# A recurrent attention with a squared-ReLU MLP on one core: a new constant set-up, a new order of the planned work, and stores that two queues may issue

## The chip, the cores and the metric

The kernel runs on one core of one Trainium2 chip. The metric is device time in microseconds (us), the median of several executions. The profile used below is of one execution, taken on the same core; its own time and its span stand in the table further down.

## The reference

The first half is a linear recurrence per batch b and head h (4 batches, 8 heads, 768 time steps, 48 channels a head); the second half is an MLP without a bias whose activation is the square of a ReLU.

```
for t in range(S):
    cur = einsum('bhd,bhe->bhde', u[None] * kt, vt)
    y[:, :, t] = einsum('bhd,bhde->bhe', rt, state + cur)
    state = w[None, :, :, None] * state + einsum('bhd,bhe->bhde', kt, vt)
x = y.transpose(0, 2, 1, 3).reshape(B * S, H * D)     # 3072 x 384
h = x @ w_in                                          # w_in 384 x 2048
r = maximum(h, 0)
out = (r * r) @ w_out                                 # w_out 2048 x 384
```

r, k and v come in float32, and so does the output. w and u have 8 x 48 elements each.

## The kernel before, in words

Time is cut into 6 chunks of 128 steps. A unit n is one chunk c of one batch b (n = 4c + b), so there are 24 units. In a chunk the recurrence becomes matrix products: k and r are scaled by powers of w (line 417 makes the table for k, line 419 the one for r; tile krp, ops kw and rw, lines 510 to 515, recorded at the helper's line 387), transposed (tile rkT: ops trk and trr on TensorE, line 540, for units 0 to 7, a DMA transpose, line 550, after that), multiplied with each other (op am, line 608), masked to the strict lower part by VectorE (op mask, tile AT, line 643), and multiplied with v (op ym, line 665). The carried state goes through kvm (lines 561 and 568), sma and smo (lines 586 and 593 or 596) and sbo (line 600), and enters ym at line 654. The term with u is a row sum: rk = r times k, rku = rk times the spread u (tile ub), du = its sum over each head (line 525), dv = du times v; yb adds it to the product (line 682). yb is transposed to xt (op yt, line 692, or the DMA of line 707).

Two units make one MLP step j (12 steps). For each of 8 slices f of the hidden dimension, m1 (line 728) makes 256 hidden features for 256 tokens, relu (line 745 on VectorE or 747 on ScalarE) and sq (line 753 on ScalarE or 755 on GpSimd) make g, and m2 (line 762) adds g times w_out into one bank for each unit. osb copies that bank out, and st (line 776) stores it from the SP queue. In steps 0 and 1 the first two slices of m1 are cut in halves, so that the first unit of the pair need not wait for the second.

All of that is a list of operations with costs, dependences and buffers, written by `op(...)`. The function `schedule` (line 39) plays it through once, when the kernel is built, and gives out engine, order and buffers; where an operation names two engines, it picks the one that it thinks ends first. NUDGE (line 232) is a hand-kept table of names with a shift of priority, a forced engine and an earliest start in the planner's own time. Nothing of that time is left on the chip. What is left is the order of the instructions on each engine and queue, which are in-order, and the semaphores.

The planner also fills holes on TensorE: where it expects TensorE to be idle before 22 us of its own time, it puts in products of a zero tile (`warm`, lines 378 to 380; five of them, WARM0, stand at the start, the others at line 806). A filler counted as 0.2133 us.

Loads come from one SP queue in the order kt, rt, vt of unit 0, 1, 2, and so on. Weights come from GpSimd's queue in five pieces each, cast to bf16 on the way. A gate (line 497) holds the first piece of w_in until kt of unit 2 has landed; loads of unit 4 wait for the fourth piece of w_in, the first piece of w_out waits for kt of unit 4, and loads of unit 6 wait for the fourth piece of w_out.

The set-up, which the change touches most, is this. Three small DMAs leave ScalarE's queue: w spread over 128 partitions (tile wb, line 288), u in one row (urow, line 290), and w in one row with 16 columns of ones between heads (wrow, line 291). VectorE sets wrow, zb (the zero tile of the fillers), ones, the four krp tiles (line 370) and the state sb_all (line 371) and copies a piece of the mask (hmask, line 376). GpSimd makes an identity in bf16, one in float32 and the mask. TensorE spreads u over 128 partitions by a product of one row (op ubp, line 408: lhsT is ones, 1 x 128, rhs is urow, 1 x 384, float32) and turns w into columns by four products of one column each (op wcol, line 402), from which ScalarE makes the decay of a whole chunk (lines 426, 427, 432).

The lines of the planner's call that name its starting times:

```
free={"T": 5.0, "V": 4.2, "A": 4.4, "P": 2.3, "D": 2.6, "S": 0.75, "W": 3.2},
away=AWAY, warm_until=WARM_UNTIL, cold=10.0)
```

Of the kernel before, what the change touches and what calls it, by code (L numbers as in the profile page):

```python
# [8 lines left out]
F32 = mybir.dt.float32  # L9
# [184 lines left out]
def kernel(  # L194
# [24 lines left out]
    L = 2  # L219
# [5 lines left out]
    WARM0 = 5  # L225
    NT = 8
    NDVE, RUN = 24, 3
    NSPLIT, NADD, NPS = 0, 0, 5
    HALVES = (2, 2)
    GATES = ()  # L230
    SLACK_FROM, HOLD, STORE_WAIT, Y_WAIT, RK_WAIT = 5.0, 1.0, 1.0, 1.0, 1.0
    NUDGE = {
        "wcol": (0.0, None, 7.04), "w_in4": (0.0, None, 15.04), "w_out3": (0.0, None, 29.23), "vt10": (0.0, None, 56.63),
        "kt11": (0.0, None, 60.71), "kt12": (0.0, None, 64.77), "kt17": (0.0, None, 96.75), "rt18": (0.0, None, 100.31),
        "rt20": (0.0, None, 117.55), "rt22": (0.0, None, 128.22), "rkT0": (0.0, "A", 0.0), "rkT1": (0.0, "A", 0.0),
        "ym1": (0.0, None, 14.89), "du2": (0.0, None, 18.67), "mask3.1": (-7.2, None, 0.0), "ym3": (0.0, None, 23.39),
        "kw4": (0.0, None, 25.68), "rk4": (0.0, None, 33.21), "trr4": (17.3, None, 0.0), "sma4": (0.0, None, 31.44),
        "rk5": (0.0, "V", 0.0), "kvm5": (0.0, None, 35.92), "rw6": (0.0, None, 42.94), "dv6": (0.0, None, 50.48),
        "ym6": (11.7, None, 0.0), "yt6": (0.0, None, 53.25), "rw7": (6.0, None, 0.0), "vb7": (4.3, None, 0.0),
        "trr7": (0.0, None, 50.11), "smo7": (0.0, "V", 0.0), "rk8": (-7.6, None, 0.0), "dv8": (0.0, None, 56.17),  # L240
        "kvm8": (-11.0, None, 54.87), "rk9": (0.0, None, 59.93), "kvm10": (0.0, None, 69.63), "rku11": (0.0, None, 69.72),
        "dv11": (5.9, None, 0.0), "am12": (7.9, None, 0.0), "mask12.1": (0.0, None, 84.71), "rw13": (0.0, None, 81.56),
        "rku13": (0.0, None, 84.65), "sma13": (6.7, None, 86.7), "am13": (0.0, None, 90.34), "ym14": (0.0, None, 97.82),
        "kw15": (-8.3, "V", 0.0), "kw16": (0.0, "V", 0.0), "rku16": (0.0, "V", 109.75), "mask16.0": (0.0, None, 111.71),
        "rw17": (-34.5, "V", 0.0), "rk17": (0.0, None, 104.69), "dv17": (0.0, "V", 111.62), "rku18": (0.0, None, 116.22),
        "dv18": (0.0, None, 122.55), "am18": (13.0, None, 0.0), "du19": (11.9, None, 118.7), "sma19": (-27.3, None, 122.48),
        "smo19": (0.0, None, 130.69), "kw20": (0.0, "V", 0.0), "rw23": (0.0, None, 140.77), "relu.0.0": (0.0, None, 19.66),
        "m2.0.0.0": (0.0, None, 31.37), "sq.0.1": (0.0, None, 21.64), "m2.0.1.1": (0.0, None, 33.75),
        "m1.0.2": (0.0, None, 20.56), "relu.0.2": (5.1, None, 0.0), "sq.0.2": (0.0, "P", 0.0), "sq.0.3": (0.0, None, 23.26),
        "m2.0.0.3": (0.0, None, 37.66), "m2.0.1.3": (0.0, None, 37.32), "m1.0.4": (20.1, None, 0.0),  # L250
        "sq.0.5": (0.0, "P", 0.0), "sq.0.7": (0.0, None, 27.24), "m2.0.1.7": (-9.7, None, 40.58),
        "m2.1.1.2": (0.0, None, 48.73), "m1.1.3": (-22.7, None, 0.0), "sq.1.3": (0.0, None, 32.7),
        "m2.1.1.4": (16.3, None, 0.0), "m1.1.6": (-6.8, None, 0.0), "osb3": (0.0, None, 55.56),
# [27 lines left out]


    wb = const.tile([128, HD], F32)
    wrow = const.tile([1, H, PAD], F32)
    urow = const.tile([1, HD], F32)
    zb = const.tile([128, 512], BF16)
    ones = const.tile([1, 128], F32)
# [101 lines left out]
    def copy(dst, src):  # L389
# [5 lines left out]
        return f  # L395


    wc_p, ub_p = Buf("a"), Buf("a")

    def column_w(e):  # L400
        for p in range(NP):
# [440 lines left out]
```

## Time and profile before

| what | value |
|---|---|
| median of 7 executions | 177.79 us (177.29 to 179.92) |
| the profiled execution's own time | 178.02 us |
| its span, first to last instruction | 176.2 us |
| TensorE matmuls, busy | 167.6 us (95%), 1667 recorded |
| VectorE, ScalarE, GpSimd, busy | 131.0, 117.4, 111.1 us |
| m1 (line 728) and m2 (line 762), busy | 74.0 us and 76.3 us |
| fillers (line 380) | 25, 9.6 us busy |
| DMA | 28.27 MB, 160 GB/s over the span |

The span leaves out what lies around the program: 178.02 - 176.2 = 1.8 us in this execution. "Busy" counts the time from an instruction's start to its end; matmuls are pipelined and their ends are modelled, so a group of n equal matmuls is better read by the distance of two starts than by the length of one. A timeline line gives start and length of a run of like instructions, and in brackets how long the engine sat idle before it and what ended that wait. The name after L is a line of the kernel; a helper's line (387, 392, 394) stands for many operations, and the tiles tell which.

### The profile page before, as it was taken

The page shows a single profiled execution, that of the slowest core. Times are in us where ns is not written, and L with a number is a line of the kernel's source. Part 1 is how long each engine was busy: PE and PEld are TensorE (multiplying, and loading weights), DVE is VectorE, ACT ScalarE, POOL GpSimd, SP SyncE. Part 2 cuts the span into 40 slices and gives each one's busy share as a digit, 9 for nine tenths or more (in the row PEclk, how much of TensorE's full clock was granted, in tenths as well). Part 3 has the DMA queues.
Part 4 walks back from the last instruction along what each step waited for, and adds up shares of the span by engine and source line. Part 5 has one row for each costly group of instructions (what it writes and reads, how often), then busy time and mean ns, then how long its engine had stood idle before and what let it go on. Part 6 is the DMA issues. An engine that isn't in the chain of part 4 may idle for free.

```text
span 176.2 us, 4385 instructions
## 1 busy us (share of the span) xinstructions
PE 167.6 (95%) x1667; PEld 120.4 (68%) x1667; DVE 131.0 (74%) x244; ACT 117.4 (67%) x234; POOL 111.1 (63%) x135
## 2 busy tenths in 40 slices
PE   5899999999999999999999998899999999999990
PEld 1554878776787677677776776577676776777850
DVE  6976998796796685995699698688885685765820
ACT  2794999883788686586495794687496572744531
POOL 3067028935999999989968877384899980000200
PEclk9999999999999999999999999999999999999999
DMA  4999998998988899799798889889999953310112
GB/s 106 210 208 187 204 179 162 133 174 170 257 186 174 202 156 234 154 210 192 147 196 197 178 194 186 180 200 192 193 136 201 173 157 69 114 26 0 48 40 94
DMA packets 106198, 28.27 MB, mean 160 GB/s; under 512 B 99009, under 2 KB 106178, under 8 KB 106178
## 3 DMA queue, kind: packets, MB, share of 16 engines
q1 hardware_dynamic: 101888, 24.65, 68.8%
q0 software_dynamic: 4128, 3.15, 12.3%
q8 instruction: 13, 0.21, 0.5%
q10 hardware_dynamic: 162, 0.20, 0.4%
q14 instruction: 7, 0.06, 0.1%
HBM read 20.65 MB, written 4.72 MB: 144 GB/s over the span
## 4 chain that ended last, share of the span: by engine, by line
PE 85%; DMA 7%; DVE 2%; POOL 1%; ACT 1%; issue 0%; DVEq 0%
PE bank L762 34%; PE bank L728 33%; PE bank L608 4%; PE bank L380 3%; PE bank L540 3%; DMA rkT<-krp 3%; PE bank L665 2%; DMA wb<-in_w_dram 2%; PE bank L654 2%; DMA xt<-yb 2%; PE bank L568 1%; DVE gr L745 1%; PE bank L402 1%; PE bank L692 1%; ACT osb L392 1%; PE bank L561 1%
## 5 line engine op out<-in xcount | busy, mean ns | idle before, releaser
L762 PE MATMUL bank<-w_out_sb,g 128*128 128x384 bf16 x384 | 76.3, 326 | 0.0
L728 PE MATMUL bank<-xt,w_in_sb 128*128 128x256 bf16 (+1 forms) x600 | 74.0, 268 | 0.6 <-DMA xt<-yb 0.5
L753 ACT ACTIVATE g<-gr 128x512 bf16<-128x512 f32 x86 | 53.1, 629 | 20.1 <-DVE gr L745 18.9
L728 PEld LDWEIGHTS <-w_in_sb 128*128 128x128 bf16 x600 | 55.6, 98 | 12.1 <-issue 1.1
L745 DVE TENSOR_SCALAR gr<-bank 128x512 f32<-128x512 f32 x62 | 42.0, 689 | 17.2 <-PE bank L728 15.7
L762 PEld LDWEIGHTS <-g 128*128 128x128 bf16 x384 | 34.7, 98 | 17.0 <-ACT g L753 0.4
L643 DVE TENSOR_TENSOR AT<-bank,smask 128x512 bf16<-128x512 f32 x48 | 31.0, 683 | 5.5 <-PE bank L608 5.1
L387 POOL TENSOR_TENSOR dv<-vb,du 128x384 f32<-128x384 bf16 x22 | 18.5, 849 | 16.9 <-DVE du L525 16.9
L747 ACT ACTIVATE gr<-bank 128x512 f32<-128x512 f32 x34 | 20.1, 594 | 8.9 <-PE bank L728 7.4
L755 POOL TENSOR_TENSOR g<-gr 128x512 bf16<-128x512 f32 x10 | 10.4, 1043 | 23.2 <-DVE gr L745 19.3
L387 POOL TENSOR_TENSOR rk<-rt,kt 128x384 f32<-128x384 f32 x18 | 18.1, 1003 | 2.9 <-DVE rku L387 2.9
L387 POOL TENSOR_TENSOR krp<-rt,wr 128x384 bf16<-128x384 f32 x18 | 18.0, 1002 | 2.5 <-DVE rku L387 1.6
L682 DVE TENSOR_TENSOR yb<-bank,dv 128x384 bf16<-128x384 f32 x24 | 13.3, 554 | 7.0 <-PE bank L665 3.6
L392 ACT COPY osb<-bank 128x384 f32<-128x384 f32 x21 | 9.3, 479 | 13.5 <-PE bank L762 13.5
L387 POOL TENSOR_TENSOR rku<-rk,ub 128x384 f32<-128x384 f32 x16 | 16.0, 1000 | 1.3 <-DVE rk L387 1.0
L387 POOL TENSOR_TENSOR krp<-kt,wk 128x384 bf16<-128x384 f32 x15 | 15.0, 1003 | 2.2 <-PE bank L665 2.2
L600 ACT CAST sb_all<-sm 64x192 bf16<-64x192 f32 x40 | 13.9, 348 | 3.7 <-POOL sm L387 2.7
L392 ACT CAST vb<-vt 128x384 bf16<-128x384 f32 x24 | 12.1, 505 | 3.4 <-DMA vt<-in_v_dram 3.3
L525 DVE TENSOR_REDUCE du<-rku 128x8 f32<-128x384 f32 x24 | 12.9, 546 | 1.3 <-POOL rku L387 1.1
L586 DVE TENSOR_TENSOR sm<-bank,sm 64x192 f32<-64x192 f32 x32 | 11.2, 351 | 2.5 <-PE bank L568 2.2
L665 PE MATMUL bank<-vb,AT 128*128 128x48 bf16 x192 | 11.3, 184 | 0.0
L380 PE MATMUL bank<-zb 128*128 128x512 bf16 x25 | 9.6, 488 | 1.7 <-DVE zb L365 1.7
(65 smaller groups left out, 141.5 us busy)
## 6 DMA issues: line engine op xcount, KB each, us to landing
kt<-in_k_dram SPq DMA_DIRECT2D x24, 192.0 KB, 3.7
rt<-in_r_dram SPq DMA_DIRECT2D x24, 192.0 KB, 3.8
vt<-in_v_dram SPq DMA_DIRECT2D x24, 192.0 KB, 3.8
out_dram<-osb SPq DMA_DIRECT2D x24, 192.0 KB, 2.3
w_in_sb<-in_moe_w_in_dram POOLq DMA_DIRECT2D x3, 384.0 KB, 8.0
w_out_sb<-in_moe_w_out_dram POOLq DMA_DIRECT2D x3, 384.0 KB, 7.4
w_in_sb<-in_moe_w_in_dram POOLq DMA_DIRECT2D x2, 192.0 KB, 5.5
w_out_sb<-in_moe_w_out_dram POOLq DMA_DIRECT2D x2, 192.0 KB, 4.1
```

The source lines that it names most:

```text
L380: nc.tensor.matmul(out=banks[7], lhsT=zb[:, :128], rhs=zb, start=True, stop=True, skip_group_check=True)
L387: return lambda e: NOW[e].tensor_tensor(dst(), a(), b_(), f)
L392: nc.scalar.copy(dst(), src())
L600: halves(lambda e, rows, i, sb=sb, sm=sm: nc.scalar.copy(SM(sb)[rows, :, i, :], SM(sm)[rows])),
L643: lambda e, T=T, i=i, x=x: nc.vector.tensor_tensor(T("AT")[:, i], psv(x, NP, C), smask[:, None, :].to_broadcast([128, NP, C]), ALU.mult),
L665: nc.tensor.matmul(out=t[:, p, i, :], lhsT=T("AT")[:, i, p, :], rhs=T("vb")[:, 2 * p + i, :], start=st is None, stop=True, skip_group_chec ...
L682: lambda e, T=T, y_p=y_p: nc.vector.tensor_tensor(T("yb"), psv(y_p, HD), T("dv").rearrange("t h d -> t (h d)"), ALU.add),
L728: nc.tensor.matmul(out=out_, lhsT=w_in_sb[:, kk, (2 * f + z) * 128 : (2 * f + z + 1) * 128], rhs=rhs, start=(kk == 0), stop=(kk == NK - 1) ...
L745: nc.vector.tensor_scalar(dst, src, 0.0, None, ALU.max)
L747: nc.scalar.activation(dst, src, AF.Relu)
L753: nc.scalar.activation(dst, src, AF.Square)
L762: nc.tensor.matmul(out=psv(o_p, dm), lhsT=G()[:, 2 * f + z, i, :], rhs=w_out_sb[:, 2 * f + z, :], start=(f == 0 and z == 0), stop=(f == NH ...
```

## The change

It does five things.

1. u is spread by a product of 128 rows: urow becomes 128 x 384 and is set to zero by VectorE, then the DMA fills its first row (so that DMA now waits for the memset), and ones becomes 128 x 128.
2. The columns of w no longer come from TensorE. GpSimd makes a mask `pick` (a memset and three copies of pieces of the bf16 identity); VectorE multiplies wb by it (op pick) and sums (op wcol, 128 x 4). The DMA and the memset of wrow are gone, and so are the float32 identity and hmask.
3. sb_all is set to zero by GpSimd and no longer by VectorE. zb is the first memset of VectorE, no longer the second. ub is copied out of PSUM by VectorE, before by ScalarE.
4. A store may be issued from ScalarE's queue.
5. The planner's costs, its starting times and the whole table NUDGE are new, so the order on every engine and the choice of engine differ. Seven fillers stand at the start, and the planner takes TensorE for slow until 5.5 us of its time, before until 10. Code that was switched off (am_split and what belongs to it) is taken out.

TensorE's work is the same but for column_w (4 products fewer) and the fillers (25 become 44). The order of the new start on TensorE, with numbers of matmuls: 7 fillers, spread of u, 4 fillers, 4 transposes (k of unit 0), 3 fillers, 8 of kvm, 4 fillers, 4 transposes (r of unit 0), 1 filler, 4 transposes (k of unit 1), 2 fillers, 8 of am (unit 0), 2 fillers, 4 transposes (r of unit 1), 1 filler, 8 of kvm, 2 fillers, 8 of ym (unit 0), 1 filler, 8 of am (unit 1), 2 fillers, 4 transposes, 1 filler, 8 of kvm, 2 fillers, 3 transposes of yb (unit 0), 2 fillers, 8 of ym (unit 1), 2 fillers, then the first m1.

What moves between engines over the whole program: 9 of 24 stores from SP to ScalarE; copies of rkT from ScalarE to VectorE (7 and 1 become 3 and 5); osb on VectorE 3 become 6; relu on VectorE 62 become 65; squares on ScalarE 86 become 81, on GpSimd 10 become 15; rku on GpSimd 16 become 19.

The core of the diff:

```diff
-    WARM0 = 5
+    WARM0, COLD = 7, 5.5
...
-    wrow = const.tile([1, H, PAD], F32)
-    urow = const.tile([1, HD], F32)
+    ub = const.tile([128, H, D], F32)
+    urow = const.tile([128, HD], F32)
+    ones = const.tile([128, 128], F32)
     zb = const.tile([128, 512], BF16)
-    ones = const.tile([1, 128], F32)
     nc.scalar.dma_start(out=wb, in_=bass.AP(tensor=w.tensor, offset=w.offset, ap=[[0, 128], [1, HD]]))
-    nc.vector.memset(wrow, 1.0)
-    nc.scalar.dma_start(out=urow, in_=u.rearrange("(o h) d -> o (h d)", o=1))
-    nc.scalar.dma_start(out=wrow[:, :, :D], in_=w.rearrange("(o h) d -> o h d", o=1))
+    nc.vector.memset(zb, 0.0)
+    nc.vector.memset(urow, 0.0)
+    nc.scalar.dma_start(out=urow[:1], in_=u.rearrange("(o h) d -> o (h d)", o=1))
     nc.scalar.preload_act_table_set("natural_log_exp_and_others")
+    nc.vector.memset(ones, 1.0)
...
     nc.gpsimd.iota(iota_i, pattern=[[0, 1]], base=0, channel_multiplier=1)
-    nc.vector.memset(zb, 0.0)
-    nc.vector.memset(ones, 1.0)
...
-    nc.vector.memset(sb_all, 0.0)
     make_identity(nc, identb)
-    make_identity(nc, identf)
     make_upper_triangular(nc, smask, val=1.0, diag=False)
-    for i in range(2):
-        nc.vector.tensor_copy(hmask[i * MID : (i + 1) * MID], smask[i * MID : (i + 1) * MID, i * MID : (i + 1) * MID])
+    nc.gpsimd.memset(pick, 0.0)
+    nc.gpsimd.tensor_copy(pick[:64, :64], identb[:64, :64])
+    nc.gpsimd.tensor_copy(pick[64:, D:], identb[64:, 64 : 64 + D])
+    nc.gpsimd.tensor_copy(pick[96:, :16], identb[96:, 112:])
+    nc.gpsimd.memset(sb_all, 0.0)
...
-    o_wb = op("wb", {"W": 0.0}, -60, [], lambda e: None, lat=0.75)
-    o_row = op("row", {"W": 0.0}, -59, [], lambda e: None, lat=0.0)
-    o_ubp = op("ubp", {"T": 1.5}, -58, [o_row], spread_u, takes=[ub_p], lat=0.25)
-    o_wcol = op("wcol", {"T": 1.65}, -57, [o_ubp], column_w, takes=[wc_p], lat=0.25)
+    o_wb = op("wb", {"W": 0.0}, -60, [], lambda e: None, lat=1.45)
+    o_ubp = op("ubp", {"T": 1.45}, -58, [], spread_u, takes=[ub_p], lat=0.25)
+    o_pick = op("pick", {"V": 0.48}, -57, [o_wb],
+                lambda e: nc.vector.tensor_tensor(
+                    picked, wb.rearrange("p (q j) -> p q j", q=NP), pick[:, None, :].to_broadcast([128, NP, 2 * D]), ALU.mult))
+    o_wcol = op("wcol", {"V": 0.46}, -56, [o_pick],
+                lambda e: nc.vector.tensor_reduce(wcol, picked, axis=mybir.AxisListType.X, op=ALU.add))
...
-        nc.scalar.activation(lnc, psv(wc_p, NP), AF.Ln)
+        nc.scalar.activation(lnc, wcol, AF.Ln)
...
-            op(f"st{q['n']}", {"S": 0.38}, KM + PACE * (L + i) - 30, [o_o],
-               lambda e, osb=osb, row=row: nc.sync.dma_start(out=out[row : row + C, :], in_=make["osb"][osb.slot]),
+            op(f"st{q['n']}", {"S": 0.45, "A": 0.5}, KM + PACE * (L + i) - 30, [o_o],
+               lambda e, osb=osb, row=row: (nc.sync if e == "S" else nc.scalar).dma_start(
+                   out=out[row : row + C, :], in_=make["osb"][osb.slot]),
...
-        free={"T": 5.0, "V": 4.2, "A": 4.4, "P": 2.3, "D": 2.6, "S": 0.75, "W": 3.2},
+        free={"T": 4.2, "V": 4.2, "A": 4.6, "P": 6.3, "D": 2.6, "S": 0.75, "W": 3.2},
...
-        away=AWAY, warm_until=WARM_UNTIL, cold=10.0)
+        away=AWAY, warm_until=WARM_UNTIL, cold=COLD)
...
-            owed += o.gap * WARM_FILL / 0.2133
+            owed += o.gap * WARM_FILL / (0.4266 if o.start < COLD else 0.2133)
```

NUDGE has 125 entries before and 190 others after; it is not printed.

## Prediction

> **What bounds the kernel now.** The page comes first: who is busy, and which chain ended last.
>
> ```profile
> PE 167.6 (95%) x1667; PEld 120.4 (68%) x1667; DVE 131.0 (74%) x244; ACT 117.4 (67%) x234; POOL 111.1 (63%) x135
> DMA  4999998998988899799798889889999953310112
> PE 85%; DMA 7%; DVE 2%; POOL 1%; ACT 1%; issue 0%; DVEq 0%
> ```
>
> TensorE is 95% busy and holds 85% of the chain. The DMA row says that from about 4 to 40 us (a slice is 4.4 us) the DMA engines have no slack either. But 95% is not 95% of useful work, so the next view is TensorE's timeline of the first 26 us.
>
> ```profile
> 1.72 2.31 PE L380 MATMUL bank<-zb 128*128 128x512 bf16 x5 [1.72 <-DVE zb L365]
> 4.34 1.61 PE L408 MATMUL bank<-urow,ones 1*128 1x384 f32 x2 [0.31 <-DMA urow<-in_u_dram]
> ...
> 7.08 1.86 PE L402 MATMUL bank<-ones,wrow 1*128 1x1 f32 x8
> 8.87 0.61 PE L540 MATMUL bank<-identb,krp 128*128 128x128 bf16 x4
> ...
> 10.15 0.63 PE L380 MATMUL bank<-zb 128*128 128x512 bf16 x1
> ...
> 12.99 1.46 PE L380 MATMUL bank<-zb 128*128 128x512 bf16 x3
> 14.39 0.61 PE L608 MATMUL bank<-rkT 48*128 48x128 bf16 x8
> ...
> 15.18 1.24 PE L380 MATMUL bank<-zb 128*128 128x512 bf16 x5
> ...
> 18.44 0.50 PE L728 MATMUL bank<-xt,w_in_sb 128*128 128x128 bf16 x6
> ...
> 22.52 0.38 PE L380 MATMUL bank<-zb 128*128 128x512 bf16 x1
> ```
>
> Three fillers in 1.46 us, where one lasts 0.63, stand 0.42 us apart; five in 1.24, where one lasts 0.38, stand 0.215 apart. So TensorE ran at half speed until about 15 us. The first MLP product starts at 18.44. The busy time before that is fillers (7.9 us), small products and column_w. After that there is little to win: the waits view of TensorE sums to under 2 us once the start is left out.
>
> ```profile
> PE bank L608 <- DMA rkT<-krp: 1.1, 2, 0.8
> PE bank L728 <- DMA xt<-yb: 0.5, 1, 0.5
> ```
>
> So what the change can give lies in the first 28 us. There VectorE is the other engine on the path; its timeline, then GpSimd's:
>
> ```profile
> 4.30 1.34 DVE L371 MEMSET sb_all<- 128x1536 uint32 x1 [0.27 <-issue]
> ...
> 11.79 1.29 DVE L643 TENSOR_TENSOR AT<-bank,smask 128x512 bf16<-128x512 f32 x2 [0.62 <-PE bank L608]
> ...
> 15.10 0.69 DVE L643 TENSOR_TENSOR AT<-bank,smask 128x512 bf16<-128x512 f32 x1 [1.56 <-PE bank L608]
> 15.71 0.55 DVE L682 TENSOR_TENSOR yb<-bank,dv 128x384 bf16<-128x384 f32 x1
> ```
>
> ```profile
> 10.88 3.24 POOL L475 DMA_DIRECT2D w_in_sb<-in_moe_w_in_dram  x4 [1.42 <-DVE rku L387]
> ```
>
> VectorE stood 1.56 us for the am of unit 1, which was itself queued behind three slow fillers (12.99 to 14.39). From 16.2 to 27.3 (yb of unit 3) it works almost without a hole.
>
> **What the Trainium skill says.** "TensorE: Matmul & The Clock Gate", Part 1: TensorE starts at half clock and gets the full clock after a window of some 3.4 us in which it was busy enough; the window runs freely. The trace agrees on both speeds (0.42 and 0.215 us). It also shows that five fillers, then products of one row, then transposes didn't suffice before 15 us. "SBUF — State Buffer", Who interferes with whom: a VectorE instruction with two SBUF inputs contends with a GpSimd one only if that reads SBUF; the moved memset doesn't read. The trace before has no such pair at the start. "DMA: Bandwidth & Descriptors", Issuing engines are not separate DMA queues: a second issuing engine saves issue time alone. Here a store costs SP 0.33 to 1.17 us of issue, median 0.46.
>
> **The change part by part.**
>
> Columns of w. Removed: column_w, 1.79 us of TensorE (7.08 to 8.87), the wrow memset (0.48) that kept zb and so the fillers waiting, and one DMA. Added: a VectorE multiply of 128x384 (0.47, the distance of like rows at 5.93, 6.40, 6.87) and a reduce (0.5, from du). VectorE can begin once wb has landed (4.73: issue 0.74 plus 4.0) and is through at 5.7. kw of unit 0 waits anyway for ScalarE's table wk, which ends at 5.89. So this costs nothing. The cover is 0.2 us; if `pick` were later than 4.9, each microsecond would go to the chain.
>
> The memsets. VectorE loses sb_all (1.34) and hmask (0.3) and gains urow (384 elements at the 0.53 us for 512 of krp: 0.40). GpSimd, free from 2.5 to 8.6 before, gets pick (about 0.8 by its 0.2 to 0.3 us rows) and sb_all, 3072 elements. No row shows that one. Ends: 1.34 us, VectorE's time for the same bytes, and 4.8, 24 times GpSimd's 0.20 for 128 elements; "GPSIMD Engine Reference", 4.1, calls one-input work roughly line-rate, which at that page's 1.2 GHz is 2.6 us, an estimate, and I take it. GpSimd is free at 5.9 (4.6 to 8.1). Its first task, rku of unit 0, has its inputs at about 7.4 and is asked for at 10.5, below. Hidden at both ends.
>
> Start of TensorE. zb comes first: fillers from 1.23, not 1.72; seven at 0.42 end at 4.2. u's DMA waits for its memset: issue about 1.7 instead of 1.23, landing plus 3.1 as before = 4.8. The spread takes 1.61 at half clock, to 6.4, now with all 128 rows. From 1.23 to 6.4 TensorE has one hole of 0.6 us. I take the full clock from 6.5 (ends: 4.8 and 8.2, one window apart).
>
> The queue from there, fillers at 0.215 and small groups as after 17 us (0.33): 4 fillers to 7.3, k transposes 7.6, 3 fillers 8.3, kvm 8.6, 4 fillers 9.5, r transposes 9.8 (before 9.4: column_w's place is given to fillers). rkT copy on VectorE, 0.65, to 10.5 (before on ScalarE, 1.01, 10.5). Then du and rw of unit 1 (0.97): mask of unit 0 at 11.5, before 11.79. Here comes the gain: r of unit 1 transposed by 11.95, rkT copied by ScalarE (1.01) to 13.1, ym of unit 0 13.3, am of unit 1 at 13.5 instead of 14.39. Its masks end at 15.2 instead of 16.8, and yb of unit 0 starts at 13.6 instead of 15.71. From 13.9 TensorE has five fillers and two small groups (1.7) before it transposes yb at 15.6, then two fillers, ym of unit 1 and two fillers: first m1 at 17.0 instead of 18.44, **-1.45**. w_in is issued about 1 us later (dv of unit 0 is ahead of it on GpSimd), but its DMA is limited by the rate, and its first piece took 5.1 us.
>
> VectorE after xt of unit 0 (done 16.2, before 17.05) has 5 products at 0.47, 3 du 0.5, 2 rkT 0.65, 2 yb 0.46, 1 sm 0.27, 4 masks and 2 relu at 0.6: 9.9 us, so yb of unit 3 at 26.1 instead of 27.27, **-1.1**. It can't be much under 25.4: kw of unit 4 is ahead of it, whose kt was issued at 22.16 and takes 2.7 at the least. I take **-1.3** for the start, carried to the end because TensorE has hardly a wait after 28 us.
>
> The rest. 9 stores off SP free 9 x 0.46 = 4.1 us of its queue, in which a store waiting for osb also holds the transposes behind it; those cost TensorE 1.1 + 0.5 us above. I take a third, **-0.5**. ScalarE pays 9 x 0.5 but loses 4 rkT copies (4.0) and 5 squares (2.7). The new order: **0**, between -1.5 and +2.5. The tail (last two osb, two stores from SP) is the same: 0.
>
> Sum -1.8: 178.02 becomes 176.2 for the profiled execution; the median, 0.2 lower, **176.0**.
>
> **The rivals.** *Absorbed*: weights and loads land when they did (DMA full to 40 us), VectorE's work takes its time, and TensorE has waits where it used to have fillers; or the new order's waits eat the start's gain. The full DMA row speaks for it; against it, TensorE is the one saturated after 28 us while DMA falls off only at 145. Gain 0.5: 177.3. *More*: full clock from 4.8 and VectorE at its floor (-1.9), all 1.6 us of SP-caused waits gone, order -0.7: -4.2, 173.6. *Slower, the clock doesn't come*: a place of its own. 20 fillers stand between the spread of u and the am of unit 1. At half clock each costs 0.21 more, +4.2 us on that chain: 13.5 + 4.2 = 17.7 for am instead of 14.39, +3.3 at the start, less the 0.5: a median of 180.6. Clock at 15 us, as before, gives the full price; each filler run at full clock takes 0.21 off, so it decides for slower (over 179.6) once the clock comes after about 13 us. For it: the trace before, where TensorE looked busy for 13 us and stayed slow. Against it: there only 2.3 us at once were full-size products; now some 5 are. *It does nothing of the kind*: the spread of u could go without moving the clock at all; then this last price holds.
>
> **How the numbers follow.** The forecast (-1 to -3, 174.8 to 176.8) 45%, absorbed 27%, more 13%, slower by the clock or by new waits of the order 15%. This measurement can tell about 1% from no change: 1.78 us, which is 176.0 and 179.6. Half of the forecast and all of "more" are beyond it, with part of the rest: faster 0.48, same 0.38, slower 0.14. For 8 in 10 the range takes in "more" and part of the slower case: 173.3 to 179.4.
>
> **What would show it.** Right: fillers 0.215 apart before 8 us, am of unit 1 near 13.5, first m1 near 17, yb of unit 3 near 26, and the last m2 some 1.5 to 2 us before 172. Wrong: fillers 0.42 apart beyond 9 us; `pick` or GpSimd's rku late with VectorE waiting; or an early start whose lead is gone by 60 us, which would put the cause in the order or the DMA.

## The result and the profile after

The changed kernel takes 179.49 us (median), the kernel before 177.79: ratio 1.0095, 95% interval 1.0068 to 1.0122. It is slower by about 1%, where 176.0 was predicted, and just beyond the upper end of the range (179.4). The profiled execution took 179.94 us with a span of 178.1, against 178.02 and 176.2. All ratios below are against the kernel before on the same chip; a ratio leaves out executions that took over 1.5% more than the fastest of their kernel, so it isn't always the quotient of two medians, and a kernel that scatters upward looks better by its ratio than by the median of all its executions.

First the page of the changed kernel: busy times, the slices of TensorE and of its clock, and the chain that ended last by engine and by line.

```profile
PE 169.3 (95%) x1678; PEld 120.6 (68%) x1678; DVE 137.8 (77%) x257; ACT 108.8 (61%) x216; POOL 117.2 (66%) x139
PE   7998999899999999999999599999999999999990
PEclk9999999999999999999999969999999999999999
DMA  4999989999989977699698999769799761300202
PE 83%; DMA 9%; POOL 3%; DVE 1%; issue 1%; ACT 0%; ACTq 0%; POOLq 0%
PE bank L702 33%; PE bank L736 33%; PE bank L397 4%; PE bank L621 4%; DMA w_out_sb<-in_moe_w_out_dram 3%; DMA w_in_sb<-in_moe_w_in_dram 3%; DMA rkT<-krp 3%; PE bank L648 2%; PE bank L643 2%; PE bank L581 1%; PE bank L553 1%; POOL g L729 1%; PE bank L418 1%; PE bank L666 1%; POOL rku L404 1%
```

The busy share is still 95%. New is what stands between: w_in and w_out have 3% of the chain each, and slices 23 and 24 (98 to 107 us) show a hole in TensorE and, after it, a clock of 0.6. TensorE's waits say the same:

```profile
PE bank L621 <- DMA rkT<-krp: 1.8, 1, 1.8
PE bank L397 <- DVE zb L306: 1.2, 1, 1.2
PE bank L702 <- DMA w_in_sb<-in_moe_w_in_dram: 0.8, 2, 0.6
PE bank L736 <- DMA w_out_sb<-in_moe_w_out_dram: 0.6, 1, 0.6
```

Now TensorE's timeline after, to 22 us (L397 fillers, L418 spread of u, L553 transposes of k or r, L621 am, L666 transpose of yb, L702 m1):

```profile
1.19 3.17 PE L397 MATMUL bank<-zb 128*128 128x512 bf16 x7 [1.19 <-DVE zb L306]
4.48 1.62 PE L418 MATMUL bank<-urow,ones 128*128 128x384 f32 x2
...
7.51 0.81 PE L397 MATMUL bank<-zb 128*128 128x512 bf16 x3
...
13.25 0.40 PE L621 MATMUL bank<-rkT 48*128 48x128 bf16 x8
...
17.26 0.51 PE L702 MATMUL bank<-xt,w_in_sb 128*128 128x128 bf16 x6 [0.63 <-DMA w_in_sb<-in_moe_w_in_dram]
...
18.41 0.51 PE L702 MATMUL bank<-xt,w_in_sb 128*128 128x128 bf16 x6 [0.20 <-DMA w_in_sb<-in_moe_w_in_dram]
...
19.20 1.03 PE L397 MATMUL bank<-zb 128*128 128x512 bf16 x4
20.15 0.31 PE L574 MATMUL bank<-vb,krp 128*64 128x48 bf16 x8
20.39 0.34 PE L666 MATMUL bank<-identb,yb 128*128 128x128 bf16 x3
...
21.32 0.40 PE L621 MATMUL bank<-rkT 48*128 48x128 bf16 x8
```

To the first m1 the forecast holds almost step by step in this execution: fillers 0.215 apart by 7.5, am of unit 1 at 13.25, first m1 at 17.26 instead of 18.44. But what follows isn't what follows before. The same stretch of the kernel before, as far as the prediction didn't show it:

```profile
18.77 0.33 PE L692 MATMUL bank<-identb,yb 128*128 128x128 bf16 x3
...
19.38 0.50 PE L728 MATMUL bank<-xt,w_in_sb 128*128 128x128 bf16 x6
19.81 0.31 PE L561 MATMUL bank<-vb,krp 128*64 128x48 bf16 x8
20.05 0.84 PE L728 MATMUL bank<-xt,w_in_sb 128*128 128x128 bf16 x12
```

Before, yb of unit 1 is transposed at 18.77, and by 20.9 the first two slices of m1 are done for both units of the pair. After, its transpose stands behind the k of unit 3, four fillers and kvm of unit 3, at 20.39; no m1 starts between 18.41 and 21.65, and then the second half of the pair is still to do. ScalarE shows the price of that place: its copy of xt waited 2.98 us for the transpose, with nothing to do.

```profile
20.77 0.48 ACT L409 COPY xt<-bank 128x384 bf16<-128x384 bf16 x1 [2.98 <-PE bank L666]
```

To see what becomes of a lead, I add up each kernel's TensorE products without fillers, each at what it takes at full clock (0.056, 0.109 and 0.163 us for 128, 256 and 384 columns, as both traces have it), and read off when a profiled execution has got through the same amount. The kernel before does about 0.3 us more (the columns of w), so for the changed kernel, f2 and xf2 a lag of about 0.3 is level; c, j, i2 and y keep the columns on TensorE, and their level is 0. The sum is an estimate, good to some 0.3 us. Lags in us behind the kernel before:

| work done, us | before, at | after | c | f2 | xf2 | j | i2 | y |
|---|---|---|---|---|---|---|---|---|
| 5 | 20.25 | 1.59 | -0.47 | 2.08 | 1.05 | 2.39 | -0.33 | -0.09 |
| 10 | 26.77 | 0.25 | -0.47 | 1.00 | 0.87 | 2.39 | -0.33 | 1.34 |
| 20 | 37.60 | 1.09 | -0.46 | 1.56 | 1.17 | 2.43 | -0.33 | 1.40 |
| 40 | 58.25 | 0.93 | 0.00 | 1.44 | 1.03 | 2.52 | -0.33 | 1.41 |
| 75 | 95.38 | 0.41 | 1.00 | 0.83 | 0.43 | 3.46 | 0.64 | 1.14 |
| 85 | 105.60 | 3.78 | 1.00 | 1.31 | 1.07 | 3.65 | 4.72 | 1.14 |
| 145 | 168.99 | 2.11 | 1.06 | 1.12 | 0.40 | 2.14 | 3.21 | 1.40 |

(The other columns are experiments, below.) After 20 us of work the changed kernel is 1.1 us behind (0.8 past level). By 95 us the lag has come down to 0.4, which is level. Then it loses 3.4 us near 100 us, gets some of that back near 110, where the kernel before has a hole of its own, and ends 2.1 behind (1.8 past level). So two places are to be explained, 17 to 34 us and 99 to 107 us; and in this pair of profiles the second accounts for nearly all that is left at the end.

### The profile page after: what moved, and what is told of

It reads as the page before. It is cut to its first block, busy times and chain, and to the rows that moved or that the text cites. A ratio compares the mean times of both kernels' runs of the same rounds, so it can differ in the third digit from the quotient of the medians.

```text
span 178.1 us, 4401 instructions
## 1 busy us (share of the span) xinstructions
PE 169.3 (95%) x1678; PEld 120.6 (68%) x1678; DVE 137.8 (77%) x257; ACT 108.8 (61%) x216; POOL 117.2 (66%) x139
## 3 DMA queue, kind: packets, MB, share of 16 engines
HBM read 20.65 MB, written 4.72 MB: 142 GB/s over the span
## 4 chain that ended last, share of the span: by engine, by line
PE 83%; DMA 9%; POOL 3%; DVE 1%; issue 1%; ACT 0%; ACTq 0%; POOLq 0%
PE bank L702 33%; PE bank L736 33%; PE bank L397 4%; PE bank L621 4%; DMA w_out_sb<-in_moe_w_out_dram 3%; DMA w_in_sb<-in_moe_w_in_dram 3%; DMA rkT<-krp 3%; PE bank L648 2%; PE bank L643 2%; PE bank L581 1%; PE bank L553 1%; POOL g L729 1%; PE bank L418 1%; PE bank L666 1%; POOL rku L404 1%
## 5 line engine op out<-in xcount | busy, mean ns | idle before, releaser
L702 PE MATMUL bank<-xt,w_in_sb 128*128 128x256 bf16 (+1 forms) x600 | 75.5, 271 | 1.0 <-DMA w_in_sb<-in_moe_w_in_dram 0.8
L702 PEld LDWEIGHTS <-w_in_sb 128*128 128x128 bf16 x600 | 56.2, 99 | 14.1 <-DMA w_in_sb<-in_moe_w_in_dram 1.6
L727 ACT ACTIVATE g<-gr 128x512 bf16<-128x512 f32 x81 | 49.6, 628 | 20.8 <-DVE gr L719 19.7
L719 DVE TENSOR_SCALAR gr<-bank 128x512 f32<-128x512 f32 x65 | 44.0, 688 | 14.0 <-PE bank L702 11.7
L721 ACT ACTIVATE gr<-bank 128x512 f32<-128x512 f32 x31 | 18.4, 596 | 12.0 <-PE bank L702 9.7
L404 POOL TENSOR_TENSOR rku<-rk,ub 128x384 f32<-128x384 f32 x19 | 19.0, 1000 | 4.0 <-DVE ub L411 1.7
L729 POOL TENSOR_TENSOR g<-gr 128x512 bf16<-128x512 f32 x15 | 15.6, 1040 | 8.4 <-ACT gr L721 4.2
L404 POOL TENSOR_TENSOR dv<-vb,du 128x384 f32<-128x384 bf16 x20 | 16.5, 829 | 6.0 <-DVE du L538 6.0
L404 POOL TENSOR_TENSOR krp<-kt,wk 128x384 bf16<-128x384 f32 x17 | 17.0, 999 | 2.3 <-DVE rku L404 0.9
L397 PE MATMUL bank<-zb 128*128 128x512 bf16 x44 | 14.7, 434 | 1.2 <-DVE zb L306 1.2
L404 POOL TENSOR_TENSOR krp<-rt,wr 128x384 bf16<-128x384 f32 x14 | 13.9, 998 | 1.8 <-DVE sm L404 0.8
L404 POOL TENSOR_TENSOR sm<-sm,wc 128x192 f32<-128x192 f32 x11 | 6.9, 627 | 8.1 <-DVE dv L404 6.9
```

Source lines behind the costliest of these rows:

```text
L397: nc.tensor.matmul(out=banks[7], lhsT=zb[:, :128], rhs=zb, start=True, stop=True, skip_group_check=True)
L404: return lambda e: NOW[e].tensor_tensor(dst(), a(), b_(), f)
L702: nc.tensor.matmul(out=out_, lhsT=w_in_sb[:, kk, (2 * f + z) * 128 : (2 * f + z + 1) * 128], rhs=rhs, start=(kk == 0), stop=(kk == NK - 1) ...
L719: nc.vector.tensor_scalar(dst, src, 0.0, None, ALU.max)
L721: nc.scalar.activation(dst, src, AF.Relu)
L727: nc.scalar.activation(dst, src, AF.Square)
```

## The experiments

Names such as kt16 or rkT15 are an operation and its unit; "ahead of" and "behind" mean the order in which the program gives the instructions out. Edits after the planner use one helper, `move(names, first)`, which takes operations out of the finished order and puts them in front of `first`. A ratio is followed by its interval.

**First theories: SyncE's queue takes the lead, or the stop near 100 us.** The rkT of unit 15 is asked for at 96.07, behind a store and three loads in SyncE's queue (93.31 to 95.96), and lands at 100.92. Four kernels: a takes the three loads away from in front of it, b asks for w_in sooner, c gives the order of before the new start, d leaves out the 128-row product.

```diff
 a: after
+    move(["kt16", "rt16", "vt16"], "relu.5.6")
 b: after
+    move(["dv0"], "w_in2")
 c: before
-    WARM0 = 5
+    WARM0 = 7
...
+    urow = const.tile([128, HD], F32)
+    ones = const.tile([128, 128], F32)
+    nc.vector.memset(zb, 0.0)
+    nc.vector.memset(urow, 0.0)
...
-    nc.vector.memset(sb_all, 0.0)
+    nc.gpsimd.memset(sb_all, 0.0)
 d: after
-        nc.tensor.matmul(out=psv(ub_p, HD), lhsT=ones, rhs=urow, start=True, stop=True)
+        nc.tensor.matmul(out=psv(ub_p, HD), lhsT=ones[:1], rhs=urow[:1], start=True, stop=True)
```

c keeps the columns of w on TensorE.

> The changed kernel, with the transpose rkT of unit 15 issued by SP ahead of the three loads of unit 16. Theory (a late transpose stops TensorE for 1.8 us near 99 us, and the stop halves the clock of the window after it in about half of the executions): the wait is gone, the mean clock of the executions is 0.994 or more, the median falls by 1.5 to 2 us to about 177.7. Rival (the loss is spread over the new order, VectorE's 6.8 us more of work above all, and the clock falls for its own reasons): the wait moves elsewhere, executions at a clock of 0.985 to 0.990 stay as frequent, the median stays within 0.5 us of 179.5.

> The changed kernel, with the first two pieces of w_in issued by GpSimd ahead of dv of unit 0. Theory (the lead of the start is lost because the weights are asked for 1 us later than before): w_in issue at 10.8 instead of 11.9, first m1 at about 16.4 instead of 17.3, TensorE's waits for w_in and w_out (1.4 us together) mostly gone, median 0.5 to 1 us lower. Rival (the DMA rate alone sets when the weights are there): the first m1 comes earlier, the last piece of w_in and the w_out pieces land when they did, the median stays within 0.3 us.

> The kernel before, its order and its column_w kept, with the changed start alone: zb set first, seven fillers, the 128-row spread of u, sb_all set by GpSimd. Theory (an early clock is worth 1 to 1.7 us and is carried to the end, the new order loses it): full clock by 7 us, first m1 at 17.0 or earlier instead of 18.4, median about 176.5. Rival (the weights and VectorE take the lead back whatever the order): first m1 earlier, median within 0.4 us of the kernel before.

> The changed kernel with the spread of u as a product of one row again (the zero rows and all else stay). Theory (the 128 rows count as work for the clock): full clock one window later, at about 10.4 instead of 7.0 us, first m1 at 18 or later, median 0.5 to 1 us higher. Rival (the seven fillers and those after it are enough): clock at 7.0, no difference.

Measured: a 1.0062 (1.0022 to 1.0102), b 1.0019 (0.9994 to 1.0045), c 1.0015 (0.9990 to 1.0040), d 1.0079 (1.0049 to 1.0109). In a the wait for rkT is gone and another has its place, and a longer one for w_in shows, in TensorE's waits:

```profile
PE bank L702 <- ACT osb L409: 1.9, 1, 1.9
PE bank L702 <- DMA w_in_sb<-in_moe_w_in_dram: 1.4, 1, 1.4
```

osb was late because ScalarE, in order, stood at the cast of vt16, which now came later; in a's timeline:

```profile
102.99 0.51 ACT L409 CAST vb<-vt 128x384 bf16<-128x384 f32 x1 [4.24 <-DMA vt<-in_v_dram]
...
104.15 0.86 ACT L409 COPY osb<-bank 128x384 f32<-128x384 f32 x2
```

So a says that the stop moves on; by the median of all its executions (181.55 against 178.37) it is 1.8% up. b says that an earlier w_in helps: d, which leaves w_in as it was, is 0.6% slower than b on the same chip. How it helps, b's profile doesn't show. TensorE has no wait for w_in left, but the first m1 comes at 17.91, later than the 17.26 of the changed kernel, and the stop near 100 us is still there (2.32 us). c is the telling one: the new start in the old order gives nothing, and costs nothing. (In its profile the full clock came only at 13.3 us, so this one execution doesn't show what an early clock is worth.) Its w_in lands as late as the changed kernel's (17.28, 18.50 and 20.44 us for the first three pieces; after 17.22, 18.36 and 21.26; before 16.00, 17.66 and 19.43), and TensorE doesn't wait for it at all: in the old order both halves of the pair use the first two pieces before the third is needed. c gives up its 0.47 us at w_out, for which TensorE waits 0.29 us at 41.3, and falls behind at rkT from 79 us on (four waits, 2.6 us in all, before 1.1). d: the one-row product had the full clock from 10.2 us instead of 6.95 in its profile, but b, with 128 rows, from 9.1, and c from 13.3: the moment varies between executions, and no gain or loss follows that can be measured.

**Is a delay carried to the end?** j holds the kernel before back by 14 fillers ahead of the first m1. f and bf are a second try at the stop, and i a first at making one. In f and bf the key scaling kw16 stands ahead of its load and reads an older unit's keys, and in i the products of unit 15 read an older rkT, so these have other values, and in i TensorE doesn't stop where it was meant to.

```diff
 f: after (bf: with b's edit too)
+    move(["kt16", "rt16", "vt16"], "kt17")
+    move(["vb16"], "sq.6.1")
 i: before
+    move(["rkT15"], "kt18")
 j: before
+        if o.name == "m1a.0.0":
+            warm(14)
```

> The changed kernel, with the loads kt16, rt16 and vt16 put behind rkT15 and xt13 in SyncE's queue, and the cast vb16 put behind the eviction osb11 on ScalarE, so that neither the transposes nor the eviction are late near 100 us. Theory New order (one stop of some 2 us near 100 us, and in about half of the executions a stretch of 3.4 us at half clock behind it, cost the gain): the wait at the product of L621 and the one at L702 are both under 0.5 us, no half-clock stretch follows, the median is 176.5 to 177.5. Rival Absorbed (transposes, loads and stores of SyncE's queue set the pace from 60 to 140 us): the stop turns up elsewhere after 100 us and the median is 178 to 179.5.

> The kernel of f, with dv0 also put behind the first two pieces of w_in on GpSimd. Theory New order: first m1 without a wait, and with no stop near 100 us the lead of about 1 us reaches the end: 175.5 to 176.8. Rival Absorbed: 177.5 to 178.8, the lead gone by 140 us at the latest.

> The kernel before, with the transpose rkT15 put behind xt13 and the loads kt17, rt17 and vt17 in SyncE's queue, which makes TensorE stop for 2 to 3 us near 100 us. If a stop brings a half-clock stretch by itself: the mean clock of about half or more of the executions falls below 0.994 (the kernel before: 2 of 75), and the median is 3 to 4.5 us above before. If the clock has another cause: mean clock stays at 0.998, and the median is at most 2.5 us above before.

> The kernel before, with 14 more products of zeros (3.0 us at full clock) put on TensorE ahead of the first m1, so that all that TensorE does from 18.4 us on comes 3 us later. If TensorE's work after the start sets the end (the step of the prediction that carries the start to the end): 2.5 to 3.2 us above before. If SyncE's queue and the transfers set the pace later on: under 1.5 us above.

Measured: f 1.0204 (1.0133 to 1.0275), bf 1.0211 (1.0148 to 1.0274), i 1.0027 (0.9987 to 1.0067), j 1.0127 (1.0080 to 1.0174). f's stop turned up at 103.8 us, behind yb, which stood 2.71 us for dv14, queued on GpSimd behind work on unit 16's late loads. i tells nothing, as the stop didn't come. j decides: 3.0 us of delay cost 2.3 us (1.4 to 3.1), and in the table it is 2.4 to 2.5 us behind from 20 to 58 us and 2.1 at the end. That is against SyncE's queue as the pace. TensorE sets the end, and in the order of before most of what is lost at the start is paid for at the end. The prediction was right in that; its sign was wrong.

**Does the stop cost the clock?** i2 makes the stop in the kernel before, k fills it in the changed kernel with zero products, bk adds b's edit, and e puts the nine stores back on SyncE.

```diff
 i2: before
+    move(["rkT15"], "rt17")
 k: after (bk: with b's edit too)
         def am(e, T=T, at=at, n=n):
+            for _ in range(8 if n == 15 else 0):
+                nc.tensor.matmul(out=psv(at[0], 512), lhsT=zb[:, :128], rhs=zb, start=True, stop=True, skip_group_check=True)
 e: after
-               lambda e, osb=osb, row=row: (nc.sync if e == "S" else nc.scalar).dma_start(
+               lambda e, osb=osb, row=row: nc.sync.dma_start(
```

> The kernel before, with the transpose rkT15 put behind xt13 and kt17 in SyncE's queue (1.9 us of issuing), and still ahead of all that read it: TensorE stops for 1.5 to 2.5 us near 100 us. If such a stop brings the half-clock stretch: the mean clock falls below 0.994 in a third of the executions or more, and the median is 1.5 to 4 us above before. If it doesn't: the mean clock stays at or above 0.994 in nearly all (the kernel before: 73 of 75), and the median is at most 2 us above before.

> The changed kernel, with eight products of zeros (1.7 us) put on TensorE ahead of the eight products of rkT of unit 15, into the bank that these then overwrite: TensorE works through the time in which it waits for the transpose, and no transfer and no other engine is touched. If the stop near 100 us is what brings the half-clock stretch, and the stretch is what makes the change slower: the mean clock is at least 0.994 in nearly all executions (the changed kernel: 13 of 25), and the median is 177.9 to 178.4, the time before. If the stretch has another cause (the early grant that is lost again at the start, say): about half of the executions stay below 0.994, and the median is 179.3 to 180.

> The kernel of k, with dv0 put behind the first two pieces of w_in on GpSimd as in b. Theory New order: 177.0 to 178.0, a little below before, as neither the wait for w_in nor the half-clock stretch is left, though the stop of some 2 us stays. Rival (the stretch isn't from the stop): 178.5 to 179.2, as b.

> The changed kernel with every store issued by SyncE at its place in the order, as in the kernel before. The prediction's 0.5 us (a third of the waits behind SyncE's queue): 0.3 to 1 us slower than the changed kernel. If SyncE's queue is the pace from 60 to 140 us: 1.5 us slower or more. If the order alone decides: the same within 0.3 us.

Measured: i2 1.0224 (1.0161 to 1.0286), with the mean clock below 0.994 in 5 of 6 executions; k 1.0103 (1.0039 to 1.0168), below in none of 6; bk 1.0048 (1.0016 to 1.0081), below in 2 of 19; e 1.0116 (1.0034 to 1.0199). In i2's timeline the am of unit 15 comes after a hole of 2.67 us:

```profile
103.14 0.61 PE L608 MATMUL bank<-rkT 48*128 48x128 bf16 x8 [2.67 <-DMA rkT<-krp]
```

The windows view gives busy times and, in the third column from the end, the mean granted clock. Of i2, and then of the changed kernel:

```profile
95.00:102.00 7.00, 5.47 (x59) 3.65 (x56) 3.92 (x8) 3.69 (x8) 5.25 (x6) 1.00 0.92 186
102.00:107.00 5.00, 3.86 (x31) 2.92 (x32) 2.39 (x5) 1.23 (x2) 1.15 (x2) 0.66 0.80 193
107.00:112.00 5.00, 5.00 (x49) 3.76 (x47) 3.90 (x7) 3.36 (x7) 2.77 (x4) 1.00 0.68 142
```

```profile
95.00:102.00 7.00, 5.19 (x56) 3.08 (x55) 4.57 (x10) 2.99 (x7) 6.71 (x8) 1.00 1.07 171
102.00:107.00 5.00, 5.00 (x46) 3.98 (x43) 3.77 (x8) 1.68 (x4) 3.21 (x4) 0.66 1.21 236
107.00:112.00 5.00, 5.00 (x45) 3.52 (x44) 3.67 (x6) 2.77 (x5) 2.75 (x3) 1.00 1.03 184
```

0.66 over 5 us is 3.4 us at half clock, some 1.7 us of work. So a stop can bring a half-clock stretch, also in the order of before, where the mean clock was below 0.994 in 2 of 75 executions; with the change it is in 12 of 25. Those 12 have a median of 180.08 us, the other 13 one of 178.08, which is 0.3 us above the kernel before. Split in this way, after the fact, most of the loss lies in the executions with a low mean.

The mean alone doesn't say where the stretch lies, nor that it costs: e's profile has one from 24.75 us as well, cs's (below) has them from 9.76 and 81.44, and 16 of 22 executions of c have a low mean without being slower by their ratio. Nor does it count the slow start, for it reads 1.00 over the first 7 us of both kernels, where fillers stand 0.42 us apart.

k's forecast fell: without the stretch, its ratio isn't back at 1. But its interval comes from six executions and holds the whole loss as well as less than half of it. The time of the stop itself is still spent in k, on products of zeros. The longest wait for data in its profile, 1.35 us before the m1 at 18.69, lies at the start, where the second piece of w_in landed at 18.65. So the stretch is part of the loss, and how large a part stays open. e: stores on SyncE or on ScalarE are the same within the interval of 0.8%.

**Order or start?** cs is c with the nine stores on ScalarE, so the change without its order. m is the order without the start (the columns of w stay on VectorE). w asks for w_out sooner. f2 takes the stop away with every load ahead of its readers.

```diff
 cs: c
-               lambda e, osb=osb, row=row: nc.sync.dma_start(
+               lambda e, osb=osb, row=row, m=q["n"]: (nc.scalar if m in (4, 5, 6, 10, 11, 12, 13, 14, 19) else nc.sync).dma_start(
 m: d
-    WARM0, COLD = 7, 5.5
+    WARM0, COLD = 5, 5.5
-    nc.vector.memset(zb, 0.0)
     nc.vector.memset(urow, 0.0)
+    nc.vector.memset(zb, 0.0)
...
+    nc.vector.memset(sb_all, 0.0)
-    nc.gpsimd.memset(sb_all, 0.0)
 w: after
+    move(["w_out0", "w_out1"], "dv2")
 f2: after
+    move(["kt16", "rt16", "vt16"], "kw16")
+    move(["kw16", "rw16"], "rk16")
+    move(["vb16"], "st10")
```

> The kernel of c (the order of before with the new start) with the same nine stores issued by ScalarE as in the changed kernel: the change without its new order. If the new order is what loses: 0.5 to 1.8 us below before, as the prediction's sum had it without the order. Rival (start and stores bring nothing that TensorE can use): within 0.5 us of before.

> The changed kernel with the start of before put back (five fillers, zb set after urow, the one-row product for u, state memset on VectorE; the columns of w stay on VectorE): the new order without the new start. If the order is what loses: 1.5 us or more above before, about as the changed kernel. Rival (the start is what loses, through weights that are asked for later): within 0.7 us of before.

> The changed kernel with the first two pieces of w_out asked for some 4 us earlier on GpSimd (ahead of dv2). If the late w_out takes the lead between 28 and 34 us: no wait for w_out, TensorE 0.5 to 1 us less behind at 34 us, median 0.5 to 1 us below the changed kernel. Rival (the transfers share one rate, and what w_out gains is lost by the loads of units 4 and 5): the wait for w_out goes but another takes its place before 40 us, median as the changed kernel.

> The changed kernel with, near 95 us, the loads of unit 16 behind rkT15 and xt13 in SyncE's queue, what GpSimd does on them (kw16, rw16) behind dv14, and the cast vb16 behind osb10 and osb11 on ScalarE; each load still stands ahead of its readers. If the stop near 100 us is what costs (1.2 us net of the stop that the kernel before has some 10 us later, and the half-clock stretch): no wait over 0.7 us near 100 us, mean clock at least 0.994 in most executions, median 0 to 0.5 us above before. Rival (TensorE stops wherever the order is tight, and unit 16 is then late in its turn): a wait of 1 us or more between 100 and 115 us, and the median is 1.5 us or more above before.

Measured on one chip: cs 1.0013 (0.9980 to 1.0045), m 1.0144 (1.0091 to 1.0196), w 1.0263 (1.0205 to 1.0320), f2 1.0111 (1.0055 to 1.0166). The order alone costs what the whole change costs, or more; start and stores together, in the old order, come to nothing by their ratio. By the medians of all executions, against 177.83, cs is 0.5% and m 1.0% up. cs's profile has a stop of 2.40 us for rkT as well, at 81 us.

w is worse by far, but its profile isn't the test that it was meant to be. In it w_out is asked for no earlier than in the changed kernel (w first, then the changed kernel), and the two issues now stand ahead of dv of unit 2:

```profile
26.80 1.48 POOL L490 DMA_DIRECT2D w_out_sb<-in_moe_w_out_dram  x2
26.85 1.48 POOL L490 DMA_DIRECT2D w_out_sb<-in_moe_w_out_dram  x2
```

Its wait of 1.7 us for w_in comes before that, at 19.80, and one of 2.5 us for rkT after it, at 104.76. Why w loses 2.6% stays open.

f2 has no stop near 100 us in its profile, and its span there is 176.7; the largest wait left is 0.97 us at 108.4. It is still 1% up by its ratio: the table has it 1.4 us behind at 58 us (1.1 past level), before anything that its edit touches.

**The place itself.** In every profile of the new order, with the new start or the old, TensorE falls back between its third and fifth us of work; m's timeline has the same sequence as the changed kernel's (no m1 from 19.96 to 23.20). In the old order c doesn't. xf2 puts the second half of the first pair forward in the new order. It does so in the place of the four fillers that run there from 19.20 to 20.06 us, after yb of unit 1 has ended (19.19); the profile shows nothing that the products behind them waited for. y puts the second half back in the old order, and further than the new order does: there the transpose of yb (20.39) stands ahead of r of unit 3 (20.57) and am of unit 2 (21.32) and only m1b behind them, while in y the transpose stands behind them too. y's transpose yt1 lands in a bank that still holds half of unit 2's scores, so part of unit 2 has other values there.

```diff
 xf2: f2
+    move(["yb1", "yt1"], "trk3")
+    move(["xt1", "m1b.0.1", "m1b.0.0"], "kvm3")
+    at["kvm3"].gap = 0.0
 y: before
+    move(["yt1", "xt1", "m1b.0.0", "m1b.0.1", "relu.0.1"], "m1.0.3")
```

> The kernel of f2, with the second half of the first MLP pair put forward in the new order: yb1 and yt1 ahead of trk3, xt1 and the two products m1b ahead of kvm3 (in the place of four fillers). If that place is what takes the lead: at 5 us of TensorE's work the lag behind the kernel before falls from 1.6 to 3 us in the new order to under 0.8, at 40 us of work it is about 0.5 us (the profile of f2: 1.4), and the median is within 0.5 us of before, 1 us below f2. Rival (the pieces of w_in, which land a microsecond or two later, are the limit): the lag at 40 us of work stays at 0.9 us or more, median as f2, 1.5 to 2 us above before.

> The kernel before, with yt1, xt1, the two products m1b and relu of the first pair put behind trr3 and am2 of its order, as the new order has them; the weights are asked for as before. If that place takes the lead: 1 to 2 us of lag at 5 us of TensorE's work, carried to the end, and a median 0.8 to 2 us above before. Rival: a lag under 0.4 us and the time of before.

Measured: y 1.0142 (1.0081 to 1.0203), a loss like that of the whole change, with the weights of before. Its timeline (L692 transpose of yb, L728 m1, and then ScalarE's):

```profile
19.87 0.54 PE L608 MATMUL bank<-rkT 48*128 48x128 bf16 x8 [0.17 <-ACT rkT L392]
20.35 0.34 PE L692 MATMUL bank<-identb,yb 128*128 128x128 bf16 x3
21.89 0.83 PE L728 MATMUL bank<-xt,w_in_sb 128*128 128x128 bf16 x12 [1.20 <-ACT xt L392]
```

```profile
20.45 1.01 ACT L392 COPY rkT<-bank 128x1024 bf16<-128x1024 bf16 x1
21.36 0.48 ACT L392 COPY xt<-bank 128x384 bf16<-128x384 bf16 x1
```

TensorE stands 1.20 us for xt, whose copy stands on ScalarE behind one of rkT, and the lag of 1.4 us stays to the end, within 0.3. So a late second half can cost 1.4% by itself, but y pays for it in a wait that the changed kernel doesn't have, where fillers and other units' products fill the gap.

xf2 1.0012 (0.9978 to 1.0047): by its ratio the new order, with both places mended, is level with the old. But it scattered more than the others, and by the median of all its 22 executions (179.21, of before 178.16) it is 0.6% up, so that isn't shown. Its profile went the way of its rival: the lag at 58 us is 1.03, not 0.5, since TensorE now waits for w_in in the place of the fillers. The changed kernel, which leaves the place as it was, lags no more there (0.93).

```profile
16.64 0.51 PE L702 MATMUL bank<-xt,w_in_sb 128*128 128x128 bf16 x6 [0.92 <-DMA w_in_sb<-in_moe_w_in_dram]
...
18.98 0.51 PE L702 MATMUL bank<-xt,w_in_sb 128*128 128x128 bf16 x6 [1.40 <-DMA w_in_sb<-in_moe_w_in_dram]
```

b leaves the place, the fillers and the stop as they were, asks for w_in sooner, and is at 1.0019. So the lateness of w_in, the place of the second half and the four fillers ahead of it all bear on the start, and no run separates them.

None of the versions beats the kernel before.

## Why the prediction was wrong

**Right.** The columns of w on VectorE and GpSimd cost nothing (wcol begins at 5.23, and kw of unit 0 follows at 5.73 without a wait, 0.2 us sooner than before). GpSimd's memset took 2.66 us, estimated at 2.6, and was hidden. The full clock came at 6.95 in the profile of after (6.5), am of unit 1 at 13.25 (13.5), the first m1 at 17.26 (17.0). The rival in which the clock doesn't come didn't happen there. That it fitted so well was in part luck of the execution: a and xf2 have the same start, and in a's profile fillers stand 0.41 us apart to beyond 9 us, which the prediction named as a sign of being wrong, while in xf2's the spread of u already ran at full clock (0.88 us, not 1.62). Of a, then of xf2:

```profile
8.77 1.45 PE L397 MATMUL bank<-zb 128*128 128x512 bf16 x3
4.52 0.88 PE L418 MATMUL bank<-urow,ones 128*128 128x384 f32 x2 [0.26 <-DMA urow<-in_u_dram]
```

The first m1 came at 18.38 in a's profile and at 16.64 in xf2's.

One reading was off without effect: "no such pair at the start" leaves out VectorE's rk of unit 1 (from 9.32), which overlaps dv of unit 0 on GpSimd (8.63 to 9.46); rk took the usual 0.55 us.

**The step that failed** is the one from the first m1 to "I take -1.3 for the start, carried to the end". It went from the first m1 over VectorE's sum of work to yb of unit 3 at 26.1, and never walked TensorE's own new queue between the two. In that queue the second half of the first pair stands behind unit 3 and unit 2. What was to be 1.3 us ahead was 0.8 past level behind at 20 us of work, and yb of unit 3 came at 27.10, level with 27.27 before. By 95 us the changed kernel was level: the term that stood at -1.3 measured about 0. Of the causes at that place, a late second half can cost 1.4% (y), and an earlier w_in gives back 0.6% (b against d); their shares in the changed kernel stay open. The queue was to be had before the run; the first m1 was the wrong milestone, since one early product says nothing about the work that has been done.

**"Carried to the end"** was right for a delay in the order of before (j, y) and wrong for a lead: c's 0.47 us were gone by 58 us, at a piece of w_out that TensorE reached before it had landed.

**"The new order: 0"** was the other half of the same error. Measured, as m against cs, it is 1.3%, some 2.3 us, near the upper end that the text gave it (2.5); by the plain medians of the two (179.65 and 178.74) it is 0.9 us. It holds the start's place and the stop near 100 us, which none of the steps had. How the loss divides between these two isn't settled: in single profiles f2 is 1.0 us better than the changed kernel at the end, and its ratio isn't. In the pair of profiles that the prediction was made for, the sum of -1.8 became +1.9: the start gave about 0 instead of -1.3, the stores nothing that can be seen instead of -0.5, and the stop near 100 us with its half-clock stretch, which the 0 for the order left out, cost some 1.8 net.

**"w_in is issued about 1 us later, but its DMA is limited by the rate"**: the first piece did land 1.22 us later, and TensorE waited 0.83 us for the first two in the new order. b, which asks sooner, is 0.6% faster than d. In the old order the same lateness was free (c).

**"I take a third, -0.5"** for stores off SyncE: nothing, cs against c and e against the changed kernel, within 0.5 and 0.8%. The store of the queue that held rkT back at 93 us still came from SyncE.

**The rivals.** *Absorbed* named both mechanisms, waits in the place of fillers and a new order that eats the gain, but still left it 0.5 us; its size was off by more than 2 us. Its waits for weights show only in the first 34 us. *Slower* named new waits of the order too, but priced only the clock.

## What to carry to other kernels

A lead is worth what the bounding engine has done, not when its first product starts: walk its new queue through the whole stretch, and compare the work done at equal times. In the order of before, 3.0 us lost at the start cost 2.3 at the end (j), while a lead of 0.47 us was lost at the first transfer that wasn't ready (c). Where a change brings a new order, that order deserves its own term, and the two kernels "old order with the new parts" and "new order with the old parts" price it at once.

## What the runs showed of the hardware

- The Trainium skill, "TensorE: Matmul & The Clock Gate", Why this matters for your kernels, asks for no gap over some 3 us between bursts of products. Here TensorE went to half clock for 3.41 us soon after a gap of 1.81 us (changed kernel: gap to 100.96, half clock from 102.53), and within one of 2.67 us (i2: gap to 103.14, half clock from 102.66). A mean clock below 0.994 came in about half of the executions of the changed kernel and in 5 of 6 of i2. Gaps of 2.32 us in b's profile and 1.79 in d's had no such stretch after them. The measurement decides: a shorter stop is already a risk, not a certainty.
- With seven fillers at the start the full clock came at about 4.5 us in xf2's profile, 6.95 in the changed kernel's, 9.1 in b's, 10.05 in f2's and 13.3 in c's. Part 1 of that page puts the spread from run to run at half a microsecond, for products without holes; here, with holes between the groups, it is nearly six us between xf2 and f2, whose starts are the same.
- Eight products of zeros put into a wait (k) kept the mean clock at 0.994 or more in 6 of 6 executions, and with b's edit (bk) in 17 of 19.
- How soon w_in could be asked for varied, with the changed kernel's start and order, from 11.06 us (f) to 13.76 (a), since it stands behind dv0 on GpSimd, and that behind du on VectorE. The first piece landed at 16.17 and 17.44.
